# Splitting a fused retention and squared-ReLU kernel into two phases, with a two-level Strassen scheme in the second product

## The chip, the cores and the metric

The kernel runs on one NeuronCore of a Trainium2 chip. The metric is the device time of one execution in microseconds. One core leaves no other core to compare with. PE is TensorE (PEld its weight loads), DVE is VectorE, ACT is ScalarE, POOL is GpSimd and SP is SyncE, which here issues transfers. All data are fp32, except that the weights arrive as 64-bit floats and are rounded to fp32 by integer operations in the kernel.

## The reference

```python
# retention: batch 8, heads 8, sequence 576, head size 64
scores = scale * (q @ k.T);  ret = (scores * decay) @ v          # causal decay per head
x = ret as (4608 tokens, 512)
h = maximum(x @ w_in, 0)                                         # w_in 512 x 2048
out = (h * h) @ w_out                                            # w_out 2048 x 512
```

## The kernel before

Tokens are worked in nine blocks of 512. Chunks of 128 tokens of the retention ("attention" below) are interleaved with steps of the two products, so that PE has work while the other engines prepare the next operands. Blocks 1 to 8 compute both products with one level of Strassen's scheme in Winograd's form: seven products of half-size blocks in place of eight. Three PSUM banks a, b and c collect them; some are read in the middle of an accumulation, and a later product adds to the same bank, so the read must be finished first.

```python
PRODUCTS = (("A11","B11","a"), ("S2","T2","b"), ("S1","T1","c"), ("A12","B21","a"),
            ("S3","T3","b"), ("S4","B22","c"), ("A22","T4","b"))
OPENS = {0, 1, 2}
CLOSES = {3, 5, 6}
...
def ffn_out(n, j, tt):                       # second product, one half of 256 tokens
    left, right, to = PRODUCTS[j]
    ...
    for m in range(N_M):                     # 8 pieces of the contraction
        nc.tensor.matmul(p[:, tt, :],
                         lhsT=G[m // 2][:, G_SLOT[left], m % 2, tt * 128:(tt + 1) * 128], rhs=w2[j][:, m, :], ...)
    ...
    if j + 2 < len(PRODUCTS):
        fetch_w2(j + 2)                      # 1 MB of right operands, again in every block
    ...
    elif j == 1:
        nc.vector.tensor_tensor(c12, p, c21, op=ALU.add)      # read of bank b, before product 4 adds to it
```

The sums S1 to S4 of the squared activations are made on POOL as soon as a quarter of the first product is squared. Block 0 uses plain products, because the weights are still being rounded while it runs:

```python
def round_c(j):                              # last two steps of rounding a piece of weights: on DVE
    nc.vector.tensor_tensor(t, f32s[:, :, 0], t.bitcast(U32), op=ALU.add)
    nc.vector.scalar_tensor_tensor(t, t, 2.0 ** -20, exp_room[j % 2], op0=ALU.mult, op1=ALU.mult)
```

Of the kernel before, what the change touches and what calls it, by code (L numbers as in the profile page):

```python
# [22 lines left out]

PRODUCTS = (
# [9 lines left out]
CLOSES = {3, 5, 6}  # L34


@with_exitstack
def kernel(
# [27 lines left out]

    nc = tc.nc
# [9 lines left out]
    N_M = N_DF // 2  # L77
    N_BLK = n_tok // TOK
    N_TS = TOK // 128
# [5 lines left out]
    ld3 = ctx.enter_context(tc.tile_pool(name="ld3", bufs=3))  # L85
    ld4 = ctx.enter_context(tc.tile_pool(name="ld4", bufs=4))
    work = ctx.enter_context(tc.tile_pool(name="work", bufs=1))
    work2 = ctx.enter_context(tc.tile_pool(name="work2", bufs=2))
    x_pool = ctx.enter_context(tc.tile_pool(name="x", bufs=2))
    w2_pool = ctx.enter_context(tc.tile_pool(name="w2", bufs=2))  # L90
    o_pool = ctx.enter_context(tc.tile_pool(name="o", bufs=1))
    dram = ctx.enter_context(tc.tile_pool(name="dram", bufs=1, space=bass.MemoryType.DRAM))
    PS = bass.MemoryType.PSUM
    ps_a = ctx.enter_context(tc.tile_pool(name="ps_a", bufs=3, space=PS))
    ps_u = ctx.enter_context(tc.tile_pool(name="ps_u", bufs=1, space=PS))
    ps_f = ctx.enter_context(tc.tile_pool(name="ps_f", bufs=4, space=PS))


    wa = [const.tile([128, N_DM, 128], F32, name=f"wa{m}") for m in range(N_M)]
    wb = [const.tile([128, N_DM, 128], F32, name=f"wb{m}") for m in range(N_M)]  # L100
    ws = [const.tile([128, 3, 2, 128], F32, name=f"ws{m}") for m in range(N_M)]

    G = [const.tile([128, 7, 2, HT], F32, name=f"g{j}") for j in range(N_M // 2)]
    G_SLOT = {n: j for j, n in enumerate(("A11", "A12", "A22", "S1", "S2", "S3", "S4"))}
    W2_SLOT = {n: j for j, n in enumerate(("B11", "B21", "B22", "T1", "T2", "T4", "T3"))}
    w2_dram = dram.tile([7, 128, N_M, d_model // 2], F32, name="w2_dram")

    g_room = [G[2][:, 2 + j:4 + j, :, :] for j in (0, 2)] + [G[3][:, j:j + 2, :, :] for j in (0, 2, 4)]
    raw_room = [t.rearrange("p a b c -> p (a b c)") for t in g_room]
    exp_room = [G[2 + j][:, 6, :, :].rearrange("p a b -> p (a b)") for j in range(2)]  # L110
    N_RAW = len(raw_room)

    def g0(m):

        return G[m // 7][:, m % 7, :, :].rearrange("p a b -> p (a b)")
# [18 lines left out]

    pieces = [(wi, m, e) for wi in range(2) for m in range(N_M) for e in range(2)]
    stage = {}
# [8 lines left out]
    def piece_dst(j):  # L145
        wi, m, e = pieces[j]
        if wi == 0:
            return (wb if e else wa)[m].rearrange("p c f -> p (c f)")
        if e == 0:

            pool, tag = (o_pool, "o") if m % 3 == 2 else (w2_pool, "w2")
            stage[m] = pool.tile([128, 8, d_model // 2], F32, tag=tag, name="w2_stage")
        return stage[m][:, 2 * e:2 * e + 2, :].rearrange("p a b -> p (a b)")

    def fetch_w(j):
        if j < len(pieces) and piece_src(j).dtype != F32:
            raw = raw_room[j % N_RAW].bitcast(I64).rearrange("p (c f) -> p c f", c=N_DM)
            nc.sync.dma_start(raw, piece_src(j))
# [3 lines left out]
    halves = {}  # L162

    def round_a(j):
        t = halves[j] = piece_dst(j)
        words = raw_room[j % N_RAW].bitcast(U32).rearrange("p (n two) -> p n two", two=2)
        f32s = raw_room[j % N_RAW].rearrange("p (n two) -> p n two", two=2)
        lo, hi = words[:, :, 0], words[:, :, 1]
        exp = exp_room[j % 2].bitcast(U32)
        nc.vector.tensor_scalar(exp, hi, 20, 0x7FF, op0=ALU.logical_shift_right, op1=ALU.bitwise_and)  # L170

        nc.vector.tensor_scalar(t.bitcast(U32), hi, 0xFFFFF, 0x100000, op0=ALU.bitwise_and, op1=ALU.bitwise_or)

        nc.scalar.activation(f32s[:, :, 0], lo, AF.Copy, scale=2.0 ** -32)

        nc.scalar.activation(exp, exp, AF.Relu, bias=exp_bias[:, 0:1], scale=2.0 ** 23)

        nc.scalar.activation(f32s[:, :, 1], hi, AF.Sign, bias=exp_bias[:, 1:2], scale=-1.0)

    def round_b(j):  # L180
        f32s = raw_room[j % N_RAW].rearrange("p (n two) -> p n two", two=2)
        nc.gpsimd.tensor_tensor(exp_room[j % 2], exp_room[j % 2], f32s[:, :, 1], op=ALU.mult)

    def round_c(j):
        t = halves.pop(j)
        f32s = raw_room[j % N_RAW].rearrange("p (n two) -> p n two", two=2)
        nc.vector.tensor_tensor(t, f32s[:, :, 0], t.bitcast(U32), op=ALU.add)
        nc.vector.scalar_tensor_tensor(t, t, 2.0 ** -20, exp_room[j % 2], op0=ALU.mult, op1=ALU.mult)

    def sum_w_out(m):  # L190

        b11, b12, b21, b22, t1, t2, t4, t3 = (stage[m][:, j, :] for j in range(8))
        nc.vector.tensor_tensor(t1, b12, b11, op=ALU.subtract)
        nc.vector.tensor_tensor(t3, b22, b12, op=ALU.subtract)
        nc.vector.tensor_tensor(t2, b22, t1, op=ALU.subtract)
        nc.vector.tensor_tensor(t4, b21, t2, op=ALU.subtract)

    def keep_w_out(m):
        nc.sync.dma_start(w2_dram[0, :, m, :], stage[m][:, 0, :])
        nc.sync.dma_start(w2_dram[1:7, :, m, :].rearrange("o p d -> p o d"), stage[m][:, 2:8, :])  # L200
# [3 lines left out]
    def prepare():  # L204

        j = n_made[0]
        if j > len(pieces):
            return
        n_made[0] += 1
        wide = piece_src(0).dtype != F32  # L210
        if j < len(pieces):
            if wide:
                round_a(j)
                round_b(j)
            else:
                nc.sync.dma_start(piece_dst(j).rearrange("p (c f) -> p c f", c=N_DM), piece_src(j))
        j -= 1
        if j >= 0:
            if wide:
                round_c(j)  # L220
                fetch_w(j + N_RAW)
            wi, m, e = pieces[j]
            if wi == 1 and m > 0 and e == 0:
                keep_w_out(m - 1)
            if wi == 1 and e == 1:
                sum_w_out(m)
                if m == N_M - 1:
                    keep_w_out(m)

    dq = const.tile([128, HP, S], F32, name="dq")  # L230
    dv = const.tile([128, H, NCH], F32, name="dv")
# [6 lines left out]
    ident = const.tile([128, 128], F32, name="ident")  # L238
    make_identity(nc, ident)

    msk = const.tile([128, 1, C], F32, name="msk")
# [6 lines left out]
    u_sb = [const.tile([128, HP, 128], F32, name=f"u_sb{j}") for j in range(2)]  # L248
    for t in u_sb:
        nc.gpsimd.memset(t, 0.0)  # L250

    st = {i: {} for i in range(N_CH)}
    xT = {}
    xs = {}
    u_ps = [None]

# [34 lines left out]
    def retain(i):  # L291
# [19 lines left out]
        while at < tok + cs:  # L311
            n = at // TOK
            end = min(tok + cs, (n + 1) * TOK)
            if n not in xT:
                xT[n] = x_pool.tile([128, N_DM, TOK], F32, tag="xT", name="xT")
# [18 lines left out]
    def first_in(m):  # L334

        m, e = divmod(m, 2)
        assert 2 * m + e < n_made[0] - 1
        p = ps_f.tile([128, TOK], F32, tag="f", name="h_ps")
        w = (wb if e else wa)[m]
        for cc in range(N_DM):  # L340
            nc.tensor.matmul(p, lhsT=w[:, cc, :], rhs=xT[0][:, cc, :], start=(cc == 0), stop=(cc == N_DM - 1))  # L341
        r = g0(m + e * N_M)
        nc.scalar.activation(r, p, AF.Relu)
        nc.gpsimd.tensor_tensor(r, r, r, op=ALU.mult)

    def sum_w_in(m):

        a11, a12 = wa[m][:, 0:2, :], wa[m][:, 2:4, :]
        a21, a22 = wb[m][:, 0:2, :], wb[m][:, 2:4, :]
        s1, s2, s4 = (ws[m][:, j, :, :] for j in range(3))  # L350
        nc.gpsimd.tensor_tensor(s1, a21, a22, op=ALU.add)
        nc.gpsimd.tensor_tensor(s2, s1, a11, op=ALU.subtract)
        nc.gpsimd.tensor_tensor(s4, a12, s2, op=ALU.subtract)
        nc.gpsimd.tensor_tensor(a21, a11, a21, op=ALU.subtract)

    acc = []

    def first_out(m):

        assert 2 * N_M + 2 * m + 1 < n_made[0] - 1  # L360
        if m == 0:
            acc.extend(ps_f.tile([128, d_model], F32, tag="f", name="acc_ps") for _ in range(N_TS))
        s = stage[m]
        for e in range(2):
            for ts in range(N_TS):
                nc.tensor.matmul(acc[ts], lhsT=g0(m + e * N_M)[:, ts * 128:(ts + 1) * 128],  # L366
                                 rhs=s[:, 2 * e:2 * e + 2, :].rearrange("p a b -> p (a b)"),
                                 start=(m == 0 and e == 0), stop=(m == N_M - 1 and e == 1))
        sum_w_in(m)
        if m == N_M - 1:  # L370
# [232 lines left out]
```

## Time and profile before

| | before |
|---|---|
| time, median of 3 runs | 1096.44 us (1095.8 to 1098.88) |
| PE instructions (matmul records) | 6464 |
| matmuls of 256 columns, start to start | 216 ns |
| granted clock, mean | 0.992 |
| DMA | 122.8 MB |

How to read it: a profile's "busy" says when an engine has an instruction in flight. Matmuls overlap, so PE can be 98% busy at any pace; the pace is the distance of two starts.

The busy table by stretch (length, busy us and instructions of PE, PEld, DVE, ACT, POOL, then the granted clock, the DMA share and GB/s) shows that after 150 us nothing but PE counts, at full clock:

```profile
0.00:150.00 150.00, 129.07 (x727) 74.73 (x728) 111.67 (x149) 77.51 (x130) 80.00 (x75) 0.95 0.73 191
150.00:1097.00 947.00, 940.94 (x5738) 802.42 (x5736) 311.04 (x446) 131.12 (x253) 301.49 (x252) 1.00 0.33 99
```

### The profile page before, as it was taken

How to read it: one execution, taken by the hardware profiler on the slowest of the kernel's cores; microseconds unless marked ns; L12 is line 12 of the kernel's file. 1: busy time of each engine (PE TensorE's matmuls, PEld its weight loads, DVE VectorE, ACT ScalarE, POOL GpSimd, SP SyncE). 2: the span in 40 equal slices, each digit the busy share in tenths (PEclk: the TensorE clock that was granted, in tenths of full speed). 3: DMA queues.
4: the chain of work that ended last, by engine and by line, in shares of the span. 5: the costliest groups of instructions: out<-in, count | busy, mean ns of one | idle time of the engine just before them, and what ended most of it. 6: DMA issues, size and time to landing. Idle time of an engine off the chain costs nothing.

```text
span 1096.8 us, 15263 instructions
## 1 busy us (share of the span) xinstructions
PE 1070.0 (98%) x6464; PEld 877.1 (80%) x6464; DVE 422.7 (39%) x594; ACT 208.6 (19%) x383; POOL 381.5 (35%) x326
## 2 busy tenths in 40 slices
PE   6789999999999999999999999999999999999997
PEld 5544546888888888888888888888888888888886
DVE  3999398441144113421343124411540144213510
ACT  3665343111011002111111111110111021001100
POOL 2566468550234204531153024502441045213410
PEclk9889999999999999999999999999999999999999
DMA  9956477304521353125511461057113620233033
GB/s 247 219 160 177 106 223 202 89 10 144 187 63 29 115 177 108 30 73 154 154 30 48 144 200 25 3 149 213 47 30 115 180 85 1 77 115 116 1 115 115
DMA packets 142612, 122.78 MB, mean 112 GB/s; under 512 B 114640, under 2 KB 131024, under 8 KB 135376
## 3 DMA queue, kind: packets, MB, share of 16 engines
q1 hardware_dynamic: 139952, 112.36, 36.0%
q0 software_dynamic: 2592, 9.44, 2.1%
q8 instruction: 51, 0.84, 0.3%
q14 instruction: 17, 0.14, 0.0%
HBM read 105.01 MB, written 16.78 MB: 111 GB/s over the span
## 4 chain that ended last, share of the span: by engine, by line
PE 89%; issue 5%; DVE 4%; DMA 1%; SPq 1%; POOLq 0%; POOL 0%; DVEq 0%
PE h_b L419 15%; PE o_b L469 13%; PE h_a L419 10%; PE h_c L419 10%; PE o_a L469 9%; PE o_c L469 9%; PE acc_ps L366 5%; PE h_ps L341 3%; PE sc L279 3%; PE x_ps L306 3%; PE x_ps L302 3%; PE kT_ps L263 1%; PE qT_ps L263 1%; DVE g L170 1%; PE u_ps L323 1%
## 5 line engine op out<-in xcount | busy, mean ns | idle before, releaser
L469 PE MATMUL o_b<-w,g 128*128 128x256 f32 x768 | 172.5, 381 | 0.0
L469 PEld LDWEIGHTS o_b<-w,g 128*128 128x128 f32 x768 | 144.5, 190 | 19.9
L419 PE MATMUL h_a<-xT,wa 128*128 128x256 f32 x512 | 122.5, 382 | 0.0
L469 PE MATMUL o_c<-w,g 128*128 128x256 f32 x512 | 115.4, 381 | 0.0
L469 PE MATMUL o_a<-w,g 128*128 128x256 f32 x512 | 114.9, 381 | 0.0
L469 PEld LDWEIGHTS o_c<-w,g 128*128 128x128 f32 x512 | 96.2, 190 | 13.6
L469 PEld LDWEIGHTS o_a<-w,g 128*128 128x128 f32 x512 | 96.3, 190 | 13.3
L419 PEld LDWEIGHTS h_a<-xT,wa 128*128 128x128 f32 x512 | 95.8, 190 | 13.7
L446 POOL TENSOR_TENSOR g<-g 128x512 f32<-128x512 f32 x32 | 40.6, 1269 | 120.2 <-DVE g L427 120.2
L288 POOL TENSOR_TENSOR vs<-v_ld,dv 128x512 f32<-128x512 f32 (+1 forms) x40 | 43.9, 1097 | 102.5 <-issue 70.6
L284 DVE TENSOR_TENSOR ret<-sc,msk 128x512 f32<-128x512 f32 (+1 forms) x80 | 47.0, 628 | 79.6 <-PE sc L279 79.6
L427 DVE SCALAR_TENSOR_TENSOR g<-g 128x512 f32<-128x512 f32 x96 | 75.1, 782 | 3.3
L380 POOL DMA_DIRECT2D out_dram<-o x18 | 13.4, 746 | 176.6 <-issue 56.0
L438 POOL TENSOR_TENSOR g<-g 128x512 f32<-128x512 f32 x32 | 33.2, 1038 | 119.1 <-ACT g L437 119.1
L306 PE MATMUL x_ps<-ret,vs 128*64 128x128 f32 (+1 forms) x640 | 59.3, 277 | 7.3 <-POOL vs L288 7.3
L419 PE MATMUL h_b<-xs,wb 128*128 128x256 f32 x256 | 61.0, 381 | 0.0
L419 PE MATMUL h_c<-xT,ws 128*128 128x256 f32 x256 | 61.0, 381 | 0.0
L419 PE MATMUL h_b<-xs,ws 128*128 128x256 f32 x256 | 60.9, 381 | 0.0
L419 PE MATMUL h_c<-xs,ws 128*128 128x256 f32 x256 | 60.9, 381 | 0.0
L419 PE MATMUL h_b<-xT,wb 128*128 128x256 f32 x256 | 60.8, 380 | 0.0
L268 ACT COPY kT<-kT_ps 128x512 f32<-128x512 f32 (+1 forms) x40 | 21.7, 542 | 185.8 <-PE kT_ps L263 185.6
L366 PE MATMUL acc_ps<-w_stage,g 128*128 128x512 f32 x128 | 56.6, 596 | 0.0
(86 smaller groups left out, 1444.5 us busy)
## 6 DMA issues: line engine op xcount, KB each, us to landing
w<-w_dram SPq DMA_DIRECT2D x56, 1024.0 KB, 5.0
out_dram<-o POOLq DMA_DIRECT2D x18, 512.0 KB, 6.0
q_ld<-in_q_dram SPq DMA_DIRECT2D x32, 256.0 KB, 5.8
k_ld<-in_k_dram SPq DMA_DIRECT2D x32, 256.0 KB, 6.0
v_ld<-in_v_dram SPq DMA_DIRECT2D x32, 256.0 KB, 4.5
g<-in_moe_w_in_dram SPq DMA_DIRECT2D x16, 512.0 KB, 5.2
g<-in_moe_w_out_dram SPq DMA_DIRECT2D x16, 512.0 KB, 4.1
w_dram<-w_stage SPq DMA_DIRECT2D x8, 768.0 KB, 5.7
```

Source lines behind the costliest of these rows:

```text
L279: nc.tensor.matmul(sc[e][:cs, hp, :cs], lhsT=kT[sl, hp, :cs], rhs=qT[sl, hp, :cs], start=True, stop=True)
L284: nc.vector.tensor_tensor(r[:cs, :, :cs], sc[e][:cs, :, :cs], msk[:cs, :, :cs].to_broadcast([cs, HP, cs]), op=ALU.mult)
L288: nc.gpsimd.tensor_tensor(vs[:cs], loaded[i][2][:cs], dv[:cs, :, ci:ci + 1].to_broadcast([cs, H, D]), op=ALU.mult)
L302: nc.tensor.matmul(p[half, hp, :cs], lhsT=u_sb[ci % 2][:, hp, half], rhs=s["qT"][:, hp, :cs], start=(hp == 0), stop=False, skip_group_chec ...
L306: nc.tensor.matmul(p[half, hp, :cs], lhsT=s["vs"][:cs, 2 * hp + e, :], rhs=s["ret"][e][:cs, hp, :cs], start=(ci == 0 and hp == 0), stop=Tr ...
L341: nc.tensor.matmul(p, lhsT=w[:, cc, :], rhs=xT[0][:, cc, :], start=(cc == 0), stop=(cc == N_DM - 1))
L366: nc.tensor.matmul(acc[ts], lhsT=g0(m + e * N_M)[:, ts * 128:(ts + 1) * 128], rhs=s[:, 2 * e:2 * e + 2, :].rearrange("p a b -> p (a b)"), ...
L419: nc.tensor.matmul(p[:, mm, :], lhsT=w[:, c, :], rhs=xs[n][right][:, c, :], start=(j in OPENS and mm == 0 and c == 0), stop=(j in CLOSES a ...
L427: nc.vector.scalar_tensor_tensor(t, t, 0.0, t, op0=ALU.max, op1=ALU.mult)
L438: nc.gpsimd.tensor_tensor(g["A11"], g["A11"], g["A11"], op=ALU.mult)
L446: nc.gpsimd.tensor_tensor(g["S3"], g["A11"], g["S1"], op=ALU.subtract)
L469: nc.tensor.matmul(p[:, tt, :], lhsT=G[m // 2][:, G_SLOT[left], m % 2, tt * 128:(tt + 1) * 128], rhs=w2[j][:, m, :], start=(j in OPENS and ...
```

## The change

The intent is to cut matmul time. Phase 1 does the attention and the first product of all nine blocks (block 0 in Strassen's form too) and writes the squared activations to DRAM. Phase 2 does the second product with two levels of the scheme: 7 outer products of 7 inner products, 49 in place of 56 half-size ones. All 49 right operands are made once and stay in SBUF. An inner product has a 128x128 block as output, so its matmuls stream 128 columns instead of 256. The core of the diff, cuts marked:

```diff
+INNER = (1, 0, 2, 4, 3, 5, 6)
...
+    W = [const.tile([128, N_MQ * NP * 128], F32, name=f"w{j}") for j in range(NP)]
+    g_dram = dram.tile([N_BLK, 4, 128, N_M, HT], F32, name="g_dram")
...
-        nc.vector.scalar_tensor_tensor(t, t, 2.0 ** -20, exp_room[j % 2], op0=ALU.mult, op1=ALU.mult)
+        nc.vector.scalar_tensor_tensor(t, t.bitcast(U32), 2.0 ** -20, as_dst(j, frac), op0=ALU.mult, op1=ALU.add)
+        nc.gpsimd.tensor_tensor(t, t, as_dst(j, exp_of(j)), op=ALU.mult)
...
+    def keep_w_out(mq):                     # inner level of the right operands: eight sums in a row, then stored
+        for st_, at in ((stage[0], slice(0, 4)), (stage[1], slice(4, 7))):
+            ...
+            nc.vector.tensor_tensor(t1, b12, b11, op=ALU.subtract)
+            ...
+            nc.sync.dma_start(w2_dram[at, :, mq, :].rearrange("o p f -> p o f"), ...)
...
+    def outer_sum(n, name):                 # 128 x 2048
+        eng, a, b_, op = {
+            "S1": (nc.gpsimd, "A21", "A22", ALU.add),
+            "S2": (nc.vector, "S1", "A11", ALU.subtract),
+            "S3": (nc.gpsimd, "A11", "A21", ALU.subtract),
+            "S4": (nc.vector, "A12", "S2", ALU.subtract),
+        }[name]
+        eng.tensor_tensor(A(n, name), A(n, a), A(n, b_), op=op)
+
+    def inner_sums(n, j):                   # 128 x 512 each
+        nc.vector.tensor_tensor(s1, x21, x22, op=ALU.add)
+        nc.vector.tensor_tensor(s2, s1, x11, op=ALU.subtract)
+        nc.gpsimd.tensor_tensor(s3, x11, x21, op=ALU.subtract)
+        nc.gpsimd.tensor_tensor(s4, x12, s2, op=ALU.subtract)
...
+    def ffn_out(n, j):
+        for at, i in enumerate(INNER):
+            for m in range(N_MQ):           # 4 pieces
+                nc.tensor.matmul(p, lhsT=lhs[il][:, m, :], rhs=w_out[j][:, m, WO_SLOT[ir], :], ...)
+            if i == 0:
+                nc.scalar.copy(p1, p)
+                nc.vector.tensor_tensor(u2, sums["b"], p1, op=ALU.add)
+            elif i == 2:
+                nc.vector.tensor_tensor(p15, p, p1, op=ALU.add)
+            elif i == 4:
+                nc.vector.tensor_tensor(r22, p, p15, op=ALU.add)
+            ...
+            if at == 3:
+                inner_sums(*divmod(n * NP + j + 1, NP))
+        ...                                 # r is then combined into the outer result: 128 x 512 sums on DVE
...
+    for n in range(N_BLK):
+        for j in range(NP):
+            ...
+            elif j == 5:
+                outer_sum(n + 1, "S1")
+            elif j == 6:
+                outer_sum(n + 1, "S2")
+                outer_sum(n + 1, "S3")
+                store(n, 0)
+            ffn_out(n, j)
+            if j == 1:
+                outer_sum(n, "S4")
```

Below, "product 0 to 6" are the outer products of a block, and "group 1 to 7" the inner ones in the order of `INNER`, eight PE instructions each (4 pieces, two instructions for an fp32 matmul). "Combination" is a sum of `r` into the outer result.

## The prediction

> **What bounds the kernel now.** I read the page's busy table and slices first, then the busy table of five stretches, then the chain of work that ended last, then the timeline of single engines.
>
> The page's busy row, and its PE and clock slices:
>
> ```profile
> PE 1070.0 (98%) x6464; PEld 877.1 (80%) x6464; DVE 422.7 (39%) x594; ACT 208.6 (19%) x383; POOL 381.5 (35%) x326
> ...
> PE   6789999999999999999999999999999999999997
> ...
> PEclk9889999999999999999999999999999999999999
> ```
>
> The busy table by stretch (start:end, length, then busy us and instructions of PE, PEld, DVE, ACT, POOL, then clock, DMA share, GB/s):
>
> ```profile
> 0.00:43.60 43.60, 27.51 (x296) 23.83 (x296) 24.19 (x36) 20.05 (x35) 14.60 (x22) 0.92 1.00 243
> 43.60:118.30 74.70, 69.86 (x297) 35.03 (x298) 64.52 (x81) 44.53 (x75) 46.58 (x35) 0.95 0.65 178
> 118.30:190.00 71.70, 71.70 (x319) 37.76 (x318) 57.60 (x80) 26.42 (x44) 49.54 (x49) 1.00 0.59 170
> 190.00:1040.00 850.00, 850.00 (x5321) 736.03 (x5320) 269.34 (x390) 115.88 (x227) 263.91 (x216) 1.00 0.32 95
> ```
>
> From about 84 us PE never stops; DVE and POOL are about a third busy. So a microsecond of matmul is a microsecond of the result, and only the head has slack. Busy is no pace, though, since matmuls overlap. I take pace from a group's length in the chain and from starts in PE's timeline. First a line of the chain, then three of the timeline:
>
> ```profile
> 250.84 6.91 PE o_b L469 x32
> ```
>
> ```profile
> 104.53 0.60 PE L263 MATMUL qT_ps<-ident,q_ld 128*128 128x128 f32 x4
> 104.97 0.60 PE L263 MATMUL kT_ps<-ident,k_ld 128*128 128x128 f32 x4
> 105.41 3.60 PE L341 MATMUL h_ps<-xT,wb 128*128 128x512 f32 x8
> ```
>
> 6.91/32 = **216 ns** for 256 columns. Four 128-column instructions start 0.44 us before the next four: **109 ns** each (median start to start), each with its own weight load. 512 columns: 429 ns (same reading). An fp32 product is two instructions (1792 records for the 896 calls of line 469).
>
> **What the Trainium skill says.** "TensorE: Matmul & The Clock Gate", section Back-to-back issue gap, gives N/2.4 + 2.5 ns; here each instruction fits 2N/2.4 + 2.5 (216 and 109), so the trace agrees once a factor 2 for this fp32 form is put in. Its section LDWEIGHTS gives P/1.2, 107 ns for 128 columns: just hidden under 109. It also warns that sustained pairs at N = 128 ran slower than the isolated gap; the transposes here do not show that, but they are bursts of eight.
>
> "SBUF — State Buffer", section "SBUF: two separate sides": DVE (in a two-port mode, or with two SBUF inputs) and GpSimd take a shared port as an exclusive lock for a whole instruction. The trace agrees, in the timeline (one engine at a time):
>
> ```profile
> 26.78 1.24 POOL L288 TENSOR_TENSOR vs<-v_ld,dv 128x512 f32<-128x512 f32 x1
> 27.98 1.74 POOL L182 TENSOR_TENSOR g<-g,g 128x512 f32<-128x512 f32 x1
> 27.02 1.54 DVE L187 TENSOR_TENSOR wa<-g,wa 128x512 f32<-128x512 f32 x1
> 28.68 1.59 DVE L188 SCALAR_TENSOR_TENSOR wa<-wa,g 128x512 f32<-128x512 f32 x1
> ```
>
> The DVE ops take 0.68 to 0.69 us undisturbed; here each ends 0.55 us after POOL's op ends. DVE reads of PSUM (692 ns for 512 columns) show no such stretch.
>
> "GPSIMD Engine Reference", section 3.1: a tensor_tensor of 2048 fp32 columns takes 4497 ns on GpSimd, 2293 ns on DVE. No op here is so long; 512 columns take 1.26 us (POOL) and 0.69 us (DVE), 256 take 0.72 and 0.42, which extend to 4.5 and 2.3. I use those.
>
> **The change, part by part.**
>
> *PE.* Before: first product 1792 x 0.216 = 387.1; second 1792 x 0.216 = 387.1; block 0, plain, 256 x 0.4295 = 110.0; sum 884.1 us. After: first product for 9 blocks, 9 x 28 x 4 x 2 = 2016 x 0.216 = 435.5; second 9 x 49 x 4 x 2 = 3528 x 0.109 = 384.6; sum 820.0. Attention is unchanged. **Gain 64.1 us**, only 7/8 on eight blocks of the second product plus Strassen for block 0. Left alone: 1096.4 - 64.1 = 1032.3.
>
> *DMA.* w2 was read again for 8 blocks (57 MB, 56 loads of 1 MB); now once. Activations go out and back (38 MB each way). A 1 MB load lands in 5.0 us, and second-product blocks last 43 us: hidden.
>
> *Head.* Block 0's first product lasts 28 x 8 x 0.216 = 48 us plus 4 chunks of attention at 4.3, 65 us, as long as before. But a weight piece now costs POOL two multiplications (1.4 + 1.3) and half of four sums (1.45), with its share of squares and attention some 4.4 us, and 1.5 us of port time for DVE: 5.9 x 16 = 94 us from about 23 us, ready near 117; PE wants the last at 44 + 3/4 x 65 = 93. Loss some 24, less the 5 PE lost there before: **+18**.
>
> *Rest of phase 1.* The sums of x now come after the last square of the block before (one shared buffer, four queued DVE ops of 0.7 us against a 1.73 us first group): about 1 us x 8. Bursts of w_out work on DVE: four of some 8 us against 4.5 us of slack. **+15.**
>
> *Between the phases.* A22, S1 and S2 chained ahead of DVE's reads: **+7.**
>
> *Phase 2.* A product is 56 x 0.109 = 6.1 us, seven groups of 0.87. Group 4 accumulates in the bank of group 1, so it waits for DVE's u2, which needs groups 1 and 2 and ACT's copy: end of group 2 at 1.9 us, copy 0.27, u2 0.28 (extrapolated from 256 and 512 columns), 2.6 us against group 4's start at 2.62. **No slack**: whatever DVE does ahead of u2 stops PE. Port time per block: POOL 14 x 1.15 + 2 x 4.4 = 24.9, DVE 21 x 0.55 + 2 x 2.15 = 15.9 us; 40.8 of 42.7, 95%. I walk the queues through a block. S4 (DVE) lies behind product 1's combination and ahead of u2 of product 2: done 1.9 us late. S1 (POOL) starts as product 5 starts, just ahead of DVE's combinations; they wait 4.5 us, u2 comes 3.7 to 4.8 us late. S3 (POOL) starts with product 6; DVE's combination, then S2, wait for it: 5 to 6 us late. So up to 9 x 1.9 + 8 x 10 + 63 x 0.08 = 102 us. Some races are within 0.1 us, and a stalled PE gives the port slack, so I take 70%: **+72**.
>
> Sum: 1032 + 18 + 15 + 7 + 72 = 1144; **1140** on record.
>
> **Rivals.**
> (a) *PE stays the bound*, as the change intends: 1035 to 1065. For it: before hid DVE and POOL wholly, with 100% PE over 850 us, and the new order of products looks made to cut waiting. Against: DVE and POOL work that was spread over 1096 us is packed into 385 us, beside groups half as long.
> (b) *Shared port and DVE's queue set phase 2*, with little loss elsewhere: 1090 to 1180. For it: every stretched DVE op above. My main reading.
> (c) *N = 128 runs slower than 109 ns* because the weight load does not hide: at 120 ns 3528 x 0.011 = +39 us. Against: the transposes.
> (d) *The clock drops.* The gaps of 3 to 5 us in the head (ended at 28.1, 38.6, 77.6) were each followed by 3.4 to 6.8 us at half clock. Sixteen such gaps in phase 2 could add 20 us to (b): up to 1200.
>
> **Range and chances.** (a) with a good head is the low tail, (b) plus (d) the high one: 1060 to 1195. Faster by over 2% (below 1074.5) needs all losses under 42 us, less than my phase 2 alone: 0.20. Within 2%: 0.22. Slower: 0.58.
>
> **What would show it.** In the profile after: 3528 second-product instructions with starts 109 ns apart inside a group (else c); DVE combinations and the 128x2048 rows stretched to the end of a POOL op; PE gaps of 2 to 6 us before the fourth group of products 2, 5 and 6, released by DVE's u2, repeating each 43 to 52 us; phase 2 near 450 us; a head with PE idle behind POOL's weight work. If u2 is never late although S1 and S3 last 4.5 us, the port does not lock for a long instruction and the prediction is wrong towards (a); if S1 and S3 are much shorter than 4.5 us, likewise.

## More of the kernel before

The idle time of PE, and what ended it, is what a change has to be held against. The table of waits of the kernel before lists (waiter, released by: us in total, times, longest), and for PE it is short:

```profile
PE x_ps L306 <- POOL vs L288: 7.3, 2, 4.4
PE qT_ps L263 <- DMA q_ld<-in_q_dram: 5.7, 2, 4.1
PE kT_ps L263 <- DVE ret L284: 4.8, 1, 4.8
```

All of it lies in the head.

## The result and the profile after

The changed kernel is correct and takes **1276.4 us** (median of 4, 1275.95 to 1276.8), against 1097.54 us for the kernel before on the same chip. The ratio is 1.1631, with a 95% interval of 1.161 to 1.1651. A ratio is the mean time of one kernel's fast runs over the mean of the other's in the same rounds, so not quite the ratio of the medians. It is slower, as the prediction held more likely than not, but by 179 us and not by 43: outside the range.

The page's busy row and its slices for PE and the clock:

```profile
PE 1087.6 (85%) x8168; PEld 981.9 (77%) x8168; DVE 750.3 (59%) x1108; ACT 204.0 (16%) x443; POOL 467.3 (37%) x346
...
PE   6389979989898999999999587787878788787788
...
PEclk9689989989899999999999797989889888888889
```

PE stood at 9 in every slice but the head's and the last; now it sinks to 7 and 8 in the right half, and the clock with it. The busy table by stretch (same columns as before) names the four parts: head, rest of phase 1, the passage between the phases, and phase 2:

```profile
0.00:150.00 150.00, 112.04 (x892) 94.02 (x892) 97.78 (x132) 61.00 (x106) 101.90 (x100) 0.89 0.69 173
150.00:700.00 550.00, 519.49 (x3719) 441.08 (x3716) 288.64 (x448) 108.98 (x211) 118.16 (x102) 0.97 0.51 151
700.00:723.00 23.00, 9.14 (x35) 7.50 (x34) 9.35 (x8) 0.60 (x1) 9.73 (x4) 0.73 0.33 117
723.00:1275.00 552.00, 446.94 (x3529) 439.29 (x3528) 354.57 (x522) 33.42 (x126) 237.54 (x142) 0.90 0.24 84
```

Phase 2 takes 552 us for 3528 instructions that were priced at 385. What PE waited for, from the table of waits:

```profile
PE o_b L576 <- DVE small L581: 99.9, 27, 5.9
PE h_b L406 <- DVE room L425: 33.6, 6, 13.9
PE h_b L406 <- DVE room L380: 21.8, 6, 15.5
```

L581 is u2, the read of bank b that group 4 has to wait for. PE's timeline shows three of its waits, in products 6, 2 and 5 (start, length, then in brackets the idle time and what ended it):

```profile
903.79 2.05 PE L576 MATMUL o_b<-w,room 128*128 128x128 f32 x8 [5.07 <-DVE small L581]
...
927.38 1.13 PE L576 MATMUL o_b<-w,room 128*128 128x128 f32 x8 [2.10 <-DVE small L581]
...
953.13 2.05 PE L576 MATMUL o_b<-w,room 128*128 128x128 f32 x8 [4.81 <-DVE small L581]
```

After the two long gaps the group takes 2.05 us instead of 1.13: it runs at half clock, that is, the trace records a granted clock of 0.5 there. Why u2 was late is seen on the two other engines. DVE's timeline:

```profile
882.93 5.03 DVE L602 TENSOR_TENSOR room<-r,room 128x512 f32<-128x512 f32 x1
887.88 1.74 DVE L603 TENSOR_TENSOR room<-r,room 128x512 f32<-128x512 f32 x1
889.55 0.28 DVE L581 TENSOR_TENSOR small<-o_b,small 128x128 f32<-128x128 f32 x1
...
896.47 3.70 DVE L605 TENSOR_TENSOR room<-r,room 128x512 f32<-128x512 f32 x1
900.09 3.35 DVE L533 TENSOR_TENSOR s<-room,a 128x2048 f32<-128x2048 f32 x1
903.36 0.28 DVE L581 TENSOR_TENSOR small<-o_b,small 128x128 f32<-128x128 f32 x1
```

and POOL's:

```profile
881.68 1.27 POOL L547 TENSOR_TENSOR room<-s,room 128x512 f32<-128x512 f32 x1 [3.92 <-PE o_c L576]
882.91 4.50 POOL L533 TENSOR_TENSOR room<-a,a 128x2048 f32<-128x2048 f32 x1
887.37 1.71 POOL L546 TENSOR_TENSOR room<-room 128x512 f32<-128x512 f32 x1
893.89 1.27 POOL L547 TENSOR_TENSOR room<-room,room 128x512 f32<-128x512 f32 x1 [4.81 <-DVE room L545]
895.11 4.51 POOL L533 TENSOR_TENSOR a<-a,a 128x2048 f32<-128x2048 f32 x1
```

S1 starts on POOL at 882.91. The combination starts 0.02 us later, a sum of 0.69 us that now takes 5.03: it ends 0.55 us after S1. The next one ends 0.54 us after the small POOL sum behind S1 (L546). Only then does u2 come, 0.28 us long. At 895 the same happens with S3, and S2 (2.3 us undisturbed) still stands between. The prediction's walk through the queues had this order of events and these sizes.

**A ledger.** For each PE record I take the array as occupied for N x 0.8333 + 2.5 ns (N columns; that fits the 216 ns and the transposes' 109 ns), and add up the time from its end to the next start. This counts waits, half clock and slow pace alike. A record that gives less than zero (the small matmuls of the attention overlap) counts as zero, and the time before the first record and after the last is left out. The two sums are 66.6 us before and 309.1 after. The difference, 242.5, less the 64.1 us of matmuls saved, is 178.4; the spans of the two profiles differ by 178.1. So the ledger accounts for the whole.

| stretch of the changed kernel | lost on PE | before, same work | extra | predicted |
|---|---|---|---|---|
| head, 0 to 150 us | 56.2 | 34.0 | 22.2 | 18 |
| rest of phase 1, to 700 | 75.6 | 32.6 | 43.0 | 15 |
| between the phases, 700 to 723 | 15.9 | - | 15.9 | 7 |
| phase 2 | 161.4 | - | 161.4 | 72 |

The 32.6 us are all that the kernel before lost after 150 us; I charge them to phase 1, where the attention now is, which is a choice of accounting. By the trace's clock records PE was at half clock for 16.7 us before and for 195.8 us after, of which 114.8 in phase 2.

### The profile page after: what moved, and what is told of

It is laid out like the page before. It is cut to its first block, busy times and chain, and to the rows that moved or that the text cites. A ratio compares the mean times of both kernels' runs of the same rounds, so it can differ in the third digit from the quotient of the medians.

```text
span 1274.9 us, 19815 instructions
## 1 busy us (share of the span) xinstructions
PE 1087.6 (85%) x8168; PEld 981.9 (77%) x8168; DVE 750.3 (59%) x1108; ACT 204.0 (16%) x443; POOL 467.3 (37%) x346
## 5 line engine op out<-in xcount | busy, mean ns | idle before, releaser
L406 PE MATMUL h_b<-room,w 128*128 128x256 f32 x864 | 223.9, 405 | 55.5 <-DVE room L425 33.6
L576 PE MATMUL o_b<-w,room 128*128 128x128 f32 x1176 | 172.9, 298 | 99.9 <-DVE small L581 99.9
L576 PEld LDWEIGHTS o_b<-w,room 128*128 128x128 f32 x1176 | 156.0, 209 | 107.5 <-issue 63.3
L406 PEld LDWEIGHTS h_b<-room,w 128*128 128x128 f32 x864 | 168.5, 201 | 85.8 <-DVE room L425 35.8
L576 PE MATMUL o_c<-w,room 128*128 128x128 f32 x1008 | 144.1, 290 | 0.0
L406 PE MATMUL h_a<-room,w 128*128 128x256 f32 x576 | 140.5, 388 | 0.0
L406 PE MATMUL h_c<-room,w 128*128 128x256 f32 x576 | 138.4, 383 | 0.0
L576 PEld LDWEIGHTS o_c<-w,room 128*128 128x128 f32 x1008 | 134.9, 208 | 0.0
L406 PEld LDWEIGHTS h_a<-room,w 128*128 128x128 f32 x576 | 109.9, 194 | 16.9
L406 PEld LDWEIGHTS h_c<-room,w 128*128 128x128 f32 x576 | 107.4, 191 | 14.6
L547 POOL TENSOR_TENSOR room<-a,room 128x512 f32<-128x512 f32 x24 | 30.6, 1273 | 127.3 <-PE o_c L576 50.8
L425 DVE TENSOR_TENSOR room<-h_b,room 128x512 f32<-128x512 f32 x36 | 24.8, 689 | 72.5 <-PE h_b L406 72.5
L547 POOL TENSOR_TENSOR room<-room,room 128x512 f32<-128x512 f32 x21 | 26.6, 1268 | 100.5 <-PE o_c L576 65.4
L322 DVE TENSOR_TENSOR ret<-sc,msk 128x512 f32<-128x512 f32 (+1 forms) x80 | 47.1, 629 | 22.2 <-PE sc L317 22.2
```

The source lines that it names most:

```text
L322: nc.vector.tensor_tensor(r[:cs, :, :cs], sc[e][:cs, :, :cs], msk[:cs, :, :cs].to_broadcast([cs, HP, cs]), op=ALU.mult)
L406: nc.tensor.matmul(p[:, mm, :], lhsT=w[:, c, :], rhs=xs[n][right][:, c, :], start=(j in OPENS and mm == 0 and c == 0), stop=(j in CLOSES a ...
L547: nc.gpsimd.tensor_tensor(s4, x12, s2, op=ALU.subtract)
L576: nc.tensor.matmul(p, lhsT=lhs[il][:, m, :], rhs=w_out[j][:, m, WO_SLOT[ir], :], start=(i in OPENS and m == 0), stop=(i in CLOSES and m == ...
```

## The experiments

Theory: in phase 2, DVE's two-input sums and POOL's sums exclude each other, the outer sums stand ahead of u2 in DVE's queue, and the clock halves after the long gaps. Rivals: the clock falls because of the short groups themselves; the order of the queues alone counts and not the shared port; 128-column matmuls are slow anyhow. For the rest: GpSimd's pace in the head, bursts of weight work, and the chain between the phases. Twelve runs. Those with one round were timed twice, counting the profiled run (their readings lie within 9 us, most within 2); the effects read from them are larger, except where said. The kernel before, timed again beside each set, stayed at 1097.5 to 1098.1 us, so times of different sets can be compared.

### Without the outer sums

```diff
-            elif j == 5:
-                outer_sum(n + 1, "S1")
             elif j == 6:
-                outer_sum(n + 1, "S2")
-                outer_sum(n + 1, "S3")
                 store(n, 0)
             ffn_out(n, j)
-            if j == 1:
+            if j == 1 and n == 0:
                 outer_sum(n, "S4")
```

> Changed kernel without the sums of the outer level for blocks 1 to 8 (wrong results on purpose). Theory A: the gaps of phase 2 come from these sums ahead of VectorE's read u2, and the half clock follows the gaps. Then the 99.9 us of waits for u2 nearly vanish, the clock in phase 2 goes from 0.89 to about 1.0, phase 2 (first second-product matmul to the end, now 550 us) takes 3528 x 0.112 = 395 us plus some 10, and the time is 1120 to 1140. Theory B: the clock falls for another reason (many short groups): the waits vanish, but the clock stays near 0.9 and the time is about 1175.

1142.16 us. Its output is wrong, which doesn't matter for the time. Waits for u2 fell from 99.9 to 8.1 us, and half clock in phase 2 from 114.8 to 3.7 us. Phase 2 in the busy table:

```profile
722.00:1142.00 420.00, 406.59 (x3529) 400.23 (x3527) 271.43 (x506) 33.58 (x126) 159.34 (x126) 1.00 0.32 111
```

and its line in the table of waits:

```profile
PE o_b L576 <- DVE small L581: 8.1, 11, 2.1
```

The clock is 1.00 with the same short groups, so the groups do not lower it; the gaps do. (The time is 2 us over the expected range: groups 3 and 4 of each product still lose 0.16 us, and product 5 still waits 0.5 us for u2.) In the ledger phase 2 falls from 161.4 to 29.5: the outer sums cost **132 us**. Of these 92 are waits; the other 40, found by subtraction, went with the half clock.

### S1 and S3 as memsets of the same length

```diff
+        if n and eng is nc.gpsimd:
+            t = A(n, name)
+            nc.gpsimd.memset(t, 0.5)
+            nc.gpsimd.memset(t, 0.25)
+            nc.gpsimd.memset(t[:, 0:N_M // 2, :], 0.5)
+            return
         eng.tensor_tensor(A(n, name), A(n, a), A(n, b_), op=op)
```

> S1 and S3 on GpSimd become memsets of about the same length (three, some 4.5 us) that read no SBUF, for blocks 1 to 8 (wrong results on purpose). Theory A1, the shared port: a GpSimd instruction that reads nothing does not hold VectorE off, so the combinations of 5.0 us go back to 0.7 us, the gap at product 5 goes, that at product 6 shrinks to what S2 itself takes (about 2 us), and the time falls by 60 to 90 us to some 1185 to 1215. Theory A2, the order alone (S2 and others wait for S1's result; GpSimd's length and not the port): the combinations stay near 5 us and the time stays within 20 us of 1276.

1183.44 us, 93 less and 1.6 us below the expected range. Its output is wrong, which doesn't matter for the time. The three memsets last 1.8, 1.8 and 0.95 us. POOL's timeline, then DVE's:

```profile
961.37 1.80 POOL L535 MEMSET room<- 128x2048 f32 x1
963.22 1.81 POOL L536 MEMSET room<- 128x2048 f32 x1
```

```profile
961.39 0.69 DVE L608 TENSOR_TENSOR room<-r,room 128x512 f32<-128x512 f32 x1
962.00 0.69 DVE L609 TENSOR_TENSOR room<-r,room 128x512 f32<-128x512 f32 x1
```

The same place in the queues: POOL starts, DVE's combination starts 0.02 us later, and takes 0.69 us, not 5.03. The first combination of product 4 fell from 4.68 to 0.82 us in the mean. Product 5 went from 13.6 to 6.41 us (median), product 6 from 13.7 to 8.45; what is left there is S2's own 2.3 us ahead of u2. Only product 2 did not gain: its gap, made by S4 on DVE, is still 2.1 us, and here it was followed by half clock in seven blocks of nine (in the changed kernel in three), so that the product takes 10.2 us in place of 8.6. The length of POOL's work and the order of the queues are as before, so it is the reading of SBUF by POOL that holds DVE off. (The memsets also wait for no load; the loads had landed before S1 started, so that plays no part in a combination's length.)

### Another order of the inner products

```diff
-INNER = (1, 0, 2, 4, 3, 5, 6)
+INNER = (1, 0, 2, 3, 4, 5, 6)
```

> Right result, one line changed: the inner products run in the order 1,0,2,3,4,5,6, so that the group that overwrites what u2 reads comes one group (0.9 us) later. Theory A (u2 has no slack): each of the three gaps of a block shrinks by 0.9 us and the 0.16 us lost in groups 3 and 4 of every product go: waits for u2 from 99.9 to 70 to 80 us, 1276 - 25 - 10 = 1235 to 1250. Theory B: the read of r22, which now has 0.4 us of slack in place of 1.2, is late instead: under 15 us gained.

1212.69 us, **64 less** by one line, more than expected. Waits for u2:

```profile
PE o_b L576 <- DVE small L581: 67.6, 25, 5.3
```

Each product loses its 0.16 us no more (6.25 us in place of 6.41). The rest is clock: half clock in phase 2 fell from 114.8 to 51.4 us. The gaps did not each shrink by 0.9 us, though: those of products 2 and 5 shrank by 1.8 (2.1 to 0.3 and 4.8 to 3.0), that of product 6 stayed at 5.0, so it is in part luck that the sum came near the expected 70 to 80 us. The line did more than was meant. The inner sums, put in DVE's queue after the fourth group, now stand ahead of r22 (the read of bank b that group 7 has to wait for) in place of behind it, S1 starts earlier, and the combination beside it is stretched to 4.16 us in place of 5.03. Why product 6 gained nothing stays open. None of the eight 3.0 us gaps at product 5 was followed by half clock, while 2.1 us gaps were in seven cases of nine in the run with memsets: the length of a gap alone does not decide it. So u2 had no slack, and r22, the rival, is not late.

### The outer sums in pieces on VectorE

```diff
+    def outer_piece(n, name, k):                    # 512 of the 2048 columns
+        ...
+        nc.vector.tensor_tensor(A(n, name)[:, c, :], A(n, a)[:, c, :], A(n, b_)[:, c, :], op=op)
+    PLACED = {(0, 2): [(0, "S2", 2), (0, "S2", 3)], (0, 3): [(0, "S3", 0)], ...}   # (product, place) -> pieces
...
+            placed(n, j, at)
```

The load of A21 moves from product 1 to product 2, because S3 now reads its buffer until then.

> Right result. All outer sums on VectorE in pieces of 512 columns, each put in its queue after a read of PSUM (p15, after the inner sums, or after r12), none ahead of u2. Theory A: no wait for u2 above 1 us, phase 2 at 400 to 425 us with clock above 0.97, time 1125 to 1155. Theory B (clock falls with short groups anyway): 1175 to 1190. If VectorE is simply too loaded (its busy time in phase 2 would be some 75 to 80%), new short gaps of 0.3 to 1 us in most products, and 1150 to 1200.

1161.16 us, correct, 115 less: 6 us above the range of theory A and inside that of the overloaded DVE. The clock in phase 2 is 1.00. Waits for u2 are 24.2 us, 34 of at most 1.1 us. Products 0, 2 and 6 take 7.48, 7.15 and 7.15 us in place of 6.41: a piece put after r12 at the end of a product stands ahead of the next product's u2, so "none ahead of u2" did not hold. (Product 5's 0.5 us is there without outer sums too.)

### The sums between the phases earlier

In the changed kernel the last block's g22 waits for a chain. Its timeline, all engines:

```profile
709.71 4.49 POOL L533 TENSOR_TENSOR room<-a,a 128x2048 f32<-128x2048 f32 x1 [17.76 <-DMA a<-g_dram]
...
714.24 3.33 DVE L533 TENSOR_TENSOR s<-room,a 128x2048 f32<-128x2048 f32 x1 [12.99 <-POOL room L533]
...
718.82 0.69 DVE L425 TENSOR_TENSOR room<-h_b,room 128x512 f32<-128x512 f32 x1
...
719.56 3.78 PE L406 MATMUL h_b<-room,w 128*128 128x256 f32 x8 [13.86 <-DVE room L425]
```

A load, S1, S2 and two inner sums stand ahead of DVE's read of g22 (L425).

```diff
-    for name in A_NAMES[:3]:
+    for name in A_NAMES:
         fetch_g(0, name)
...
-        if n == N_BLK - 1 and mp == N_MP - 1 and j == 2:
-            fetch_g(0, "A22")
-            outer_sum(0, "S1")
...
+        if n == N_BLK - 1 and mp == 1 and j == 5:
+            outer_sum(0, "S1")
+        if n == N_BLK - 1 and mp == 2 and j == 2:
+            outer_sum(0, "S2")
...
```

> Right result. Between the phases: A22 of block 0 is fetched with the other three, and the outer sums of block 0 are made one to six groups earlier, each where VectorE has slack. Theory: the single gap of 13.9 us at 705 us goes (A22's load, S1 and S2 in a chain ahead of the read of g22), with some 3 us of half clock after it: 1256 to 1264. Rival: it comes back as gaps of 2 to 5 us earlier, since S1 and S3 of 4.5 us now hold the port beside the squares: 1265 to 1276.

1257.44 us, 19 less, within the expected range. The gap is gone; between 680 and 721 us PE waits nowhere longer than 0.5 us.

### The weight work in phase 1

The timeline of the changed kernel around 174 us, all engines:

```profile
174.83 2.46 SPq L228 DMA_DIRECT2D w_dram<-w  x2
...
180.90 0.43 DVE L187 TENSOR_SCALAR w<-w 128x512 uint32<-128x512 uint32 x1 [3.67 <-DMA w_dram<-w]
181.24 0.68 DVE L425 TENSOR_TENSOR room<-h_b,room 128x512 f32<-128x512 f32 x1
...
181.98 2.50 PE L406 MATMUL h_b<-room,w 128*128 128x256 f32 x5 [8.25 <-DVE room L425]
```

The next piece's second operation (L187) overwrites the staging buffer, so DVE's whole queue waits 3.67 us for the store to leave. I had counted eight sums and missed that wait.

```diff
+        if j > N_W1:
+            finish(j - 1)
+            owe_begin.append(j)              # begun four groups later
+            return
```

> Right result. While the weights of the second product are prepared, the first two VectorE operations of the next piece are put four groups later, so that they no longer wait in VectorE's queue for the store of the staging buffer that they overwrite (3.7 us each time). Theory A: the gaps of 8.4, 5.8 and 4.3 us at 174, 254 and 406 us shrink by 3.7 us each or go, with the half clock after them: 1258 to 1266. Theory B: the burst of eight sums alone makes them: under 5 us gained.

1263.37 us, 13 less, within the range of theory A. (Its gaps are counted from a matmul's end by the ledger; the profile's idle times, used here, are 0.1 to 0.2 us shorter.) The gaps of 8.25 and 5.68 us became 4.64 and 2.94; that at 406 us, after the last set, kept its 4.10. A gap of 6.14 us at 330, ended by ACT and not named in the expectation, became one of 3.28.

### The head

Two runs. The first puts the sums of the first x ahead of the weight pieces; the second also moves the last multiplication of a piece from POOL to DVE, where the kernel before has it, and issues POOL's other one earlier.

```diff
+            if i == 5:
+                sum_x(0)
```

```diff
-        nc.gpsimd.tensor_tensor(t, t, as_dst(j, exp_of(j)), op=ALU.mult)
+        nc.vector.tensor_tensor(t, t, as_dst(j, exp_of(j)), op=ALU.mult)
```

> Right result. The sums of the first block of x are put in VectorE's queue before the weight pieces instead of behind three of them. Theory A (order of the queue): the gap of 15.5 us at 43.5 us mostly goes and stays gone: 1258 to 1268. Theory B (GpSimd's pace in preparing the weights, some 5 to 6 us a piece, sets the head): the gap comes back before the second, third and fourth quarter of block 0, and under 6 us are gained.

> Right result. Sums of x ahead of the weight pieces as in the run on them alone, and the last multiplication of a weight piece moved from GpSimd to VectorE as in the kernel before, with GpSimd's first one issued a piece earlier. Theory A (GpSimd's pace, 5 to 6 us a piece, sets the head): 1.3 us a piece less on GpSimd, 1276 - 15 to 25 = 1250 to 1261, the gap of 10 us at 50 us under 4. Theory B (VectorE just takes over as the bound, with block 0's eight reads and squares a quarter on it): 1265 to 1276.

1272.88 us in two runs that differ by 8 us, so the gain is unclear. The gap of 15.5 us at 43.5 is nearly gone (1.7), but one of 9.8 us opened at 50 us and that at 75 grew from 4.2 to 6.7: the wait came back, as in theory B. The second run gives 1269.13, some 7 us in all and in the range of its theory B, and the head's loss in the ledger is 53.5 against 56.2. The gap at 50 us fell to 3.9 as in its theory A, but one of 7.8 us behind POOL's vs (the scaled v of the attention) opened at 34. So neither theory is shown cleanly. The head is set by several engines at once.

### The pace of 128-column matmuls alone

The kernel *before*, with each 256-column matmul of the second product cut in two:

```diff
+            for c in range(2):
-                nc.tensor.matmul(p[:, tt, :], ..., rhs=w2[j][:, m, :],
+                nc.tensor.matmul(p[:, tt, c * 128:(c + 1) * 128], ..., rhs=w2[j][:, m, c * 128:(c + 1) * 128],
```

> The kernel before, with each matmul of its second product (256 columns) issued as two of 128 columns on the same weights: 3584 records in place of 1792, nothing else changed. It measures the pace of long runs of 128-column fp32 matmuls without the change's queues. If the pace is 109 ns, as for the transposes and as predicted: +4 us, 1101. If it is 112 ns, as inside the groups of the changed kernel: 3584 x 0.112 - 387 = +14 us, 1112. If the weight load is a bound only in bursts or not at all, or other engines were behind the 112: 109.

1110.78 us, correct, ratio 1.0113 (1.0096 to 1.013), or 12.4 us: (387.1 + 12.4)/3584 = 111.5 ns. PE's timeline has a run of 57 that ends where the next begins, at 256.29:

```profile
249.83 6.53 PE L470 MATMUL o_b<-w,g 128*128 128x128 f32 x57
```

6.46/57 = 113 ns, the median is 112, and after the head PE waits for nothing in this kernel. So a long run of 128-column matmuls has a pace of 112 ns, not the 109 ns of the transposes. For 3528 instructions that is 10 us. A weight-load record lasts 192 ns here and 140 ns for the transposes; whether that makes the 3 ns was not tested.

### Everything together

First the pieces, the earlier sums between the phases, the later begin of pieces, the earlier sums of x and DVE's multiplication:

> Right result. The outer sums in pieces, the earlier sums between the phases, the later start of the weight pieces, the earlier sums of x, and the last multiplication of a weight piece on VectorE as in the kernel before, together. If the gains add up: 1276 - 115 - 19 - 14 - 12 = 1116, from 1105 to 1130; so still slower than the kernel before, unless the multiplication on VectorE shortens the head by more than 15 us.

1130.68 us, correct, ratio 1.0294 (1.0274 to 1.0315). It is 0.7 us above the range: 146 us were gained where the single gains sum to 160. Then, in addition, the new inner order, pieces placed after u2, r22 and r12 only, the eight sums of the second product's weights split in two halves, and POOL's multiplication a piece earlier:

> Right result, everything together: outer sums in pieces at places after u2, p15's follower and r22, the new order of inner products, the sums between the phases earlier, weight pieces and the sums of the second product's weights spread, and the head as in the run on it. Phase 2 from 435 to 400 to 412 us (floor 63 x 6.27 = 395), phase 1 from 694 to 670 to 685: 1072 to 1098, against 1098 of the kernel before: same to 2% faster. If r22 becomes the late read, phase 2 stays above 420 and the time above 1105.

**1087.00 us** (median of 4), correct, ratio 0.9894 (0.9878 to 0.9911) to the kernel before: faster than both kernels, by 1.1% over the better one, which is within the 2% that count as the same. Its busy table by stretch:

```profile
0.00:150.00 150.00, 118.59 (x947) 98.37 (x948) 112.72 (x152) 61.49 (x106) 83.56 (x83) 0.90 0.71 182
150.00:655.00 505.00, 492.25 (x3602) 418.57 (x3601) 288.31 (x451) 106.56 (x208) 101.23 (x86) 0.99 0.53 158
655.00:675.00 20.00, 20.00 (x95) 17.60 (x94) 17.68 (x18) 1.78 (x3) 11.43 (x6) 1.00 0.64 243
675.00:1086.00 411.00, 400.41 (x3530) 395.85 (x3528) 359.10 (x637) 33.40 (x126) 193.89 (x123) 1.00 0.31 113
```

Phase 2 is 411 us at clock 1.00, with DVE at 359 us (87%). Waits for u2 are 2.6 us, against 24.2 in the run with the pieces alone, where DVE was busy for 338 of 436 us (78%): the places and the order made those waits, not DVE's load. In the ledger the losses are 52.1, 47.4, 0.0 and 20.4 us. The head has hardly moved. Last, the same with the multiplication back on POOL. Its edit also puts POOL's other multiplication back to its later place, so, against its text, it differs in two things:

> Right result. The combined version with the last multiplication of a weight piece left on GpSimd, as in the changed kernel; it differs from the combined version in that alone. If GpSimd's pace in the head is what costs there: 1092 to 1100, slower than 1087, with the first product of block 0 ending later than at 132 us. If VectorE is as tight as GpSimd in the head: within 4 us of 1087. If VectorE is the tighter one: 1078 to 1083.

1092.90 us, ratio 0.9946 (0.9927 to 0.9965): 6 us worse, the expectation for GpSimd's pace. Of these, 5.1 us are lost in the head: a matmul of the first product that started at 137.98 us in the combined version starts at 143.06 here. So how much and how early POOL multiplies is one of the head's limits, though not a large one; which of the two counts is not shown.

## Why the prediction was right or wrong

- **Right: what bounds the kernel, and the matmul arithmetic.** 242.5 us lost less 64.1 saved gives the difference of the spans to 0.3 us.
- **Right: the mechanism in phase 2.** No slack at u2, S4 ahead of it in product 2, S1 in product 5, S3 and S2 in product 6. The walk gave 102 us, 97 without the 5 of groups 3 and 4; the waits for u2 sum to 99.9. The memset run shows the port, the order run the missing slack. The lengths for 2048 columns that the prediction took from the Trainium skill ("GPSIMD Engine Reference", section 3.1: 4497 ns on GpSimd, 2293 ns on DVE) are 4.50 and 2.28 us here.
- **Wrong: "I take 70%".** The argument that a stalled PE gives the port slack had no measurement behind it. The stalls recur in full: 2.1 us at product 2 in all nine blocks, 4.8 at product 5 and 4.7 to 5.9 at product 6 in the eight that have them. The trace suggests why: S1 and S3 start right behind a POOL sum (L547) that itself waited for PE (3.92 us) or for DVE (4.81 us), so a stalled PE makes them late too and no slack arises. It cost 28 us of the miss.
- **Wrong: the half clock left out of the sum.** It stood as rival (d), with 20 us, in the upper end of the range alone. It measured about 40 us in phase 2 (132 us for the outer sums less 92 of waits), from gaps that the walk itself had put at 3.7 to 6 us.
- **Wrong: 109 ns.** Rival (c) was argued away with bursts of transposes; the pace is 112 ns, for 10 us. Its reason, a weight load that does not hide, was not tested. These three, with some 10 us in groups 3 and 4 (5 in the walk, before the 70%), make phase 2's 161.4 in place of 72.
- **Wrong: the rest of phase 1**, 43.0 in place of 15. The bursts were named, but as DVE work only; the wait for the store inside DVE's queue was missed. Taking that wait away gave 13 us. Between the two combined runs, where the sums were split and POOL's multiplication came earlier, the loss of this part fell from 60.7 to 47.4 us; the remainder was not divided further.
- **Too small: between the phases**, 15.9 in place of 7, with the right chain. Undoing it gave 19 us.
- **About right in size, in part by luck: the head**, 22.2 for 18. The sum rested on POOL's pace alone, and that is not borne out: relieving it brought about 6 us. What else holds the head stays open.
- **Right: DMA is hidden**, as far as phase 2's waits show: no wait of PE in it was ended by a transfer.
- **The range** failed because its high end took (b) with 20 us of (d) and nothing of (c). All three came true together, (d) at about twice its size and (c) at a quarter of its 39 us, and phase 1 fell short as well.

## What to carry to other kernels

When two engines' sums share a port and a read of PSUM stands behind them in a queue, price the read's lateness and not the engines' busy shares: a 4.5 us sum on POOL cost PE about 5 us of waiting, and half clock after the waits added some 40% to that (40 us to 92), with DVE only 64% busy in phase 2 (355 of 552 us). Cut long elementwise work into pieces as long as the slack, and put them behind the reads that PE waits for; look at the order in which groups reuse a bank, where one line was worth 64 us. And when a walk through the queues gives a number, do not discount it without a measurement.

## What the Trainium skill lacked or had wrong

- "TensorE: Matmul & The Clock Gate", Back-to-back issue gap: it gives no pace in ns for fp32 matmuls. Here each of the two records of an fp32 matmul has a pace of 216 ns at 256 columns and of 429 at 512, which is 2N/2.4 + 2.5; at 128 columns it is 109 ns for transposes but 112 ns in long runs of ordinary matmuls.
- The same page, "The HAM clock gate": it states one idle window of about 3.4 us as what sets the clock back. Over the fourteen traces here, all 159 gaps of 4 us or more that began at full clock were followed by half clock (within 2 us of the gap's end), and so were 62 of 181 gaps of 1 to 4 us, 55 of them under 3 us. A half-clock record in the changed kernel lasted 6.8 us in 17 of 30 cases, the rest of the gap included.
- "SBUF — State Buffer", "SBUF: two separate sides": the exclusive lock, and its absence for POOL instructions that only write, agree with the traces (a 0.69 us sum stretched to 5.03, and 0.69 us beside a memset). It has no figure for how soon a DVE sum ends after the POOL sum that held it off: 0.55 us here.
